# Which engine copies and stores which half of the last output tile, in a fused attention and feed-forward kernel

## The chip, the cores and the metric

The kernel runs on one core of one Trainium2 chip. The metric is device time in microseconds (us) of one execution, the median of several. The core's engines each work through their own instructions in order and meet only through semaphores: TensorE (PE in the profile; its weight loads are PEld), VectorE (DVE), ScalarE (ACT), GpSimd (POOL) and SyncE (SP). In this kernel SP does nothing but issue stores and wait; ACT computes and, towards the end, issues stores too. A row marked ACTq or SPq is the time in which that engine issues a DMA or waits, not the transfer itself.

## The reference

```python
def _attn_ref(q, k, v):                       # each (8, 12, 448, 64), float32
    scores = scale * np.matmul(q, k.transpose(0, 1, 3, 2))
    attn = softmax(scores)
    return np.matmul(attn, v)

def _moe_ref(x, w_in, w_out):                 # x (3584, 768), w_in (768, 2048), w_out (2048, 768)
    h = x @ w_in
    g = h * (1.0 / (1.0 + np.exp(-h)))
    return (g @ w_out).astype(np.float32)
```

The output of the attention, its 12 heads laid side by side, is x. The result is 3584 rows (tokens) of 768 numbers in float32.

## The kernel before, in words

Matrices are held in 16 bits; products add up in PSUM in float32. The kernel goes batch by batch through the attention, and starts the feed-forward part of a batch as soon as its x is there. What concerns us is only the very end, the second product `g @ w_out`.

That product is done in blocks of two by two: 2 x 128 rows of g with 2 halves of the 2048 inner positions, against 2 halves of the inner positions and 2 halves of 384 output columns. A scheme with seven products in place of eight is used (numbers 1, 5, 6, 2, 7, 3, 4 in the code, in this order), each of eight steps of 128 inner positions. One such block is called a quad; there are 14 of them, and `QL` (line 785) is the last, number 13. A quad makes four output tiles of 128 x 384, named by row block and column half: 00 comes from product 2's bank, 11 after product 7, 01 after product 3, and 10 after product 4, the very last product. `product` (line 788) issues the matmuls; for `QL` this is line 799, with 128 x 128 weights.

A finished tile is copied or added from its PSUM bank into an SBUF tile of the pool `ost` (four buffers, `ost` at line 825) and stored from there. Tiles 00 and 01 are copied by ACT (`take_out`, line 862, the copy itself is line 863), 11 is an addition on DVE (`add_out`, line 880, row L881). For all quads but the last, `store` (line 842) issues four DMAs of 48 KB (line 855); near the end the second and fourth of these go through ACT, the others through SP. For the last quad `store_last` (line 830) issues one DMA for a whole tile, 192 KB, at line 837, through SP unless told otherwise.

The very last tile, 10 of quad `QL`, is made in two column halves of 192 (`OQ`, line 786). `queue_quad` (line 1297), in `run` at lines 1320 to 1329, issues product 4 as two runs of eight matmuls, one for each column half, and queues one copy for each: `take_half` (line 866). Half 0 is copied by ACT (line 872) and stored through SP; half 1 is copied by DVE (line 870) and stored through ACT. Both halves lie in one PSUM bank and in one `ost` tile. This crossing matters for what follows: ACT issues the store of the half that DVE has copied, and SP issues the store of the half that ACT has copied.

The order of the instructions on each engine comes from a planner (`Order`, line 88). It keeps a clock `od.now` and a time at which each engine is free, starts the ready operation that has waited longest (with biases), and notes for each one the moment at which it was started; at the end of the kernel function (line 1742) all operations are emitted in the order of those moments. An operation's copy and its store are emitted together, since one function does both. So the planner's clock decides in which order ACT gets the two things it has to do for the last tile: the store of DVE's half, and its own copy. In the built program of the kernel before, ACT has the DMA issue of half 1 first and the copy of half 0 behind it. The waits are put in by the framework: DVE's copy (L870) waits for the last matmul of both halves, ACT's DMA issue waits for DVE's copy, ACT's copy (L872) waits for the last matmul of half 0, and SP's last store waits for ACT's copy. After its last store SP waits for every DMA of the kernel, one semaphore after the other (row L1769), and then all engines meet.

The lines that decide this, for the last product:

```python
op = Op("PE", HF * mm(OQ), lambda h=h: product(qd, m, 0, HF, h), tail=PE_OUT)
od.now += HF * mm(OQ) * x
od.on_pe(op, "full")
eng = "DVE" if x else "ACT"
read(("21", x), eng, lambda x=x: take_half(x), [op])
```

Of the kernel before, what the change touches and what calls it, by code (L numbers as in the profile page):

```python
# [30 lines left out]
def mm(n):  # L31
    return n / 2400.0 + 0.0026


def act(n):
    return n * 0.00087 + 0.13
# [151 lines left out]
def kernel(  # L188
# [9 lines left out]
    nc = tc.nc  # L198
# [410 lines left out]
    HF = NFF // 2  # L609
# [175 lines left out]
    QL = NT * B // 4 - 1  # L785
    OQ = OH // 2

    def product(qd, m, f0, f1, h=slice(0, OH)):
        a, b = 2 * qd, 2 * qd + 1
        if m in (5, 6):  # L790
            w = S_t[(qd, m - 4)]
        else:
            t, i = {1: (a, 0), 2: (a, 1), 3: (a, 1), 7: (b, 0), 4: (b, 1)}[m]
            w = rows(t, i)
        if BANK[m] == m and f0 == 0:
            pr_t[(qd, m)] = bank_m("p", qd, m)
        for f in range(f0, f1):
            if qd == QL:
                nc.tensor.matmul(  # L799
                    out=pr_t[(qd, BANK[m])][:, h],  # L800
                    lhsT=w[:, f, :],
                    rhs=W_[m][:, f, h],
                    start=(f == 0 and BANK[m] == m),
                    stop=(f == HF - 1),
                    skip_group_check=True,
                )
                continue
            wide(
                out=pr_t[(qd, BANK[m])][:, 0:OH],
                lhsT=w[:, f, :],  # L810
                rhs=W_[m][:, f, :],
                start=(f == 0 and BANK[m] == m),
                stop=(f == HF - 1),
                skip_group_check=True,
            )


    def bank(qd, m):
        return pr_t[(qd, m)][:, 0:OH]
# [5 lines left out]
    def ost(qd, i, j):  # L825
        t = sb.tile([128, OH], FP32, name=f"ost_{qd}_{i}{j}", tag="ost", bufs=NOST)
        ost_t[(qd, i, j)] = t
        return t

    def store_last(i, j, h=slice(0, OH), eng=nc.sync):  # L830
        u, t = divmod(2 * QL + i, NT)
        r, col = divmod(128 * t, S)
        b = 2 * u + r
        dst = out[b * S : (b + 1) * S, OH * j : OH * (j + 1)].rearrange(
            "(i g) m -> i g m", g=TPP
        )
        eng.dma_start(  # L837
            out=dst[:, col // 32 : col // 32 + 4, h],
            in_=ost_t[(QL, i, j)][:, h],
        )  # L840
# [18 lines left out]
    def take(qd, m):  # L859
        nc.scalar.copy(out=tmp(qd, m), in_=bank(qd, m))  # L860

    def take_out(qd, m, i, j):
        nc.scalar.copy(out=ost(qd, i, j), in_=bank(qd, m))  # L863
        store(qd, i, j)

    def take_half(x):
        h = slice(OQ * x, OQ * (x + 1))
        t = ost_t.get((QL, 1, 0)) or ost(QL, 1, 0)
        if x:
            nc.vector.tensor_copy(out=t[:, h], in_=bank(QL, 6)[:, h])  # L870
        else:
            nc.scalar.copy(out=t[:, h], in_=bank(QL, 6)[:, h])  # L872
        store_last(1, 0, h, nc.scalar if x else nc.sync)

    def add_in(qd, to, x, y):
        nc.vector.tensor_tensor(
            out=bank(qd, to), in0=bank(qd, x), in1=tmp_t[(qd, y)], op=ALU.add
        )

    def add_out(qd, m, x, i, j):  # L880
        nc.vector.tensor_tensor(  # L881
            out=ost(qd, i, j), in0=bank(qd, m), in1=tmp_t[(qd, x)], op=ALU.add
        )
        store(qd, i, j)
# [14 lines left out]
    od = Order(SHY)  # L899
# [123 lines left out]
    def in_parts(n, size, columns, emit, done, at=0):  # L1023
        to = min(at + size, n)
        op = Op("PE", (to - at) * mm(columns), lambda: emit(at, to), tail=PE_OUT)
        od.on_pe(op, "full")
        if to == n:
            done(op)
        else:
            moe.insert(  # L1030
                0, (list, 0, lambda: in_parts(n, size, columns, emit, done, to), ())
            )
# [264 lines left out]
    def queue_quad(qd):  # L1297
        quads.append(qd)
        fourth.append(qd)
        took = {}  # L1300

        def read(name, eng, fn, deps, then=None):
            busy = act(OH) if eng == "ACT" else OH / 960.0 + 0.13
            bias = B_TAKE if eng == "ACT" else B_READ
            took[name] = od.add(Op(eng, busy, fn, deps, bias, then=then))

        def out(m):
            def then(at):
                m_ring.give(at, spot[("p", qd, m)])
                ost_ring.give(at + STORE)  # L1310

            return then

        def queue(m):
            def run():
                if BANK[m] == m:
                    spot[("p", qd, m)] = m_ring.take()[0]
                for ring, need in rings:
                    ring.take(need)
                if qd == QL and m == 4:  # L1320
                    pr_op[(qd, m)] = None
                    for x in range(2):
                        h = slice(OQ * x, OQ * (x + 1))
                        op = Op("PE", HF * mm(OQ), lambda h=h: product(qd, m, 0, HF, h), tail=PE_OUT)
                        od.now += HF * mm(OQ) * x
                        od.on_pe(op, "full")
                        eng = "DVE" if x else "ACT"
                        read(("21", x), eng, lambda x=x: take_half(x), [op])
                    return
                in_parts(HF, PROD_AT, OH, lambda f0, f1: product(qd, m, f0, f1), done)  # L1330

            def done(op):
                if m == 5:
                    sg_ring.give(od.free["PE"] + PE_OUT)
                pr_op[(qd, m)] = op
                if m in (1, 5):
                    read(m, "ACT", lambda: take(qd, m), [op])
                elif m == 6:
                    read("u", "DVE", lambda: add_in(qd, 6, 6, 1), [op, took[1]], tmp_ring.give)
                    read("w", "DVE", lambda: add_in(qd, 5, 6, 5), [took["u"], took[5]])  # L1340
                elif m == 2:
                    read("11", "ACT", lambda: take_out(qd, 1, 0, 0), [op], out(1))
                elif m == 7:
                    read(
                        "22",
                        "DVE",
                        lambda: add_out(qd, 6, 5, 1, 1),
                        [op],
                        lambda at: (ost_ring.give(at + STORE), tmp_ring.give(at)),
                    )  # L1350
                elif m == 3:
                    read("12", "ACT", lambda: take_out(qd, 5, 0, 1), [op], out(5))
                else:
                    read("21", "ACT", lambda: take_out(qd, 6, 1, 0), [op], out(6))

            def deps():
                made = list(w_op.get(m, [None]))
                made += [took.get(x) for x in {2: (1,), 7: ("w",), 3: ("w",), 4: ("22",)}.get(m, ())]
                first = {5: 1, 6: 5, 7: 6, 3: 7, 4: 3}.get(m)
                if (qd, m) == (QL - 1, 4):  # L1360
                    made.append(pr_op.get((QL, 6)))
                if first:
                    made.append((pr_op.get((qd, first)), 9.0))
                elif m == 1 and qd > 0:
                    made.append((pr_op.get((qd - 1, 1)), 9.0))
                if m in (1, 2, 4):
                    t = 2 * qd + (m == 4)
                    for b in {(128 * t + c) // S for c in (0, 127)}:
                        for f in range(HF):
                            x = g_op.get((b, f + HF * (m > 1)), [None])  # L1370
                            made += [(y, f * mm(OH)) for y in x]
                    return made + ld_wout
                x = sg_op.get((qd, {5: 1, 6: 2, 7: 3, 3: 4}[m]), [])
                x = x if len(x) == 2 else [None, None]
                return made + [x[0], (x[1], 4 * mm(OH))]

            rings = ((tmp_ring, 1),) if m in (1, 5) else ((ost_ring, 1),) * (m != 6)
            moe.append((deps, int(BANK[m] == m), run, rings))

        for m in (1, 5, 6, 2, 7, 3, 4):  # L1380
            queue(m)
# [392 lines left out]
```

## Time and profile before

| what | value |
|---|---|
| median of 3 runs | 382.96 us (382.51 to 383.04) |
| the profiled execution's own time | 383.52 us |
| its span, first to last instruction | 381.5 us |
| granted TensorE clock over the span | 0.999 |
| TensorE busy | 374.3 us, 98% |
| VectorE busy | 279.8 us, 73% |
| ScalarE busy | 257.5 us, 67% |
| GpSimd busy | 85.2 us, 22% |

The span counts from the program's first instruction to its last on the core; the execution's own time is 2.0 us more, which lies around it. Busy times are sums over the whole span. The last 5 us look nothing like the rest, so the view to read for this change is the end: which engine does what after the last matmul, and what it waits for. All times of the trace below are in us from the start of the span.

### The profile page before, as it was taken

To read this page: it belongs to the slowest core of one execution; us is meant where nothing else is said; L and a number is where in the kernel's file an instruction comes from. 1 tells how busy PE (TensorE), PEld (TensorE's weight loads), DVE (VectorE), ACT (ScalarE), POOL (GpSimd) and SP (SyncE) were. 2 spreads that over 40 slices of the span, in tenths; PEclk is the share of its full clock that TensorE was granted. 3 is DMA by queue.
4 is the path that set the end of the run, shared out by engine and by line. 5 is a ranking of instruction groups with operands and counts; after the bars stand their busy time and mean duration, and the time that the engine had idled before them with its cause. 6 is when DMAs were issued, how large, how long until landed. Compare 5 with 4: busy or idle time off the path is not lost.

```text
span 381.5 us, 12934 instructions
## 1 busy us (share of the span) xinstructions
PE 374.3 (98%) x5516; PEld 192.6 (50%) x5516; DVE 279.8 (73%) x560; ACT 257.5 (67%) x425; POOL 85.2 (22%) x155
## 2 busy tenths in 40 slices
PE   8899999999999999999999999999999999999995
PEld 7433455444455444545444454555556555556663
DVE  4679799999996868997869978789866334556341
ACT  4897864887868787967788787728762259883221
POOL 7536714506042503314240500000000000000000
PEclk9999999999999999999999999999999999999999
DMA  7999999935558842739391612120002330001333
GB/s 108 195 206 181 176 210 197 164 73 90 71 99 138 140 74 41 108 65 174 80 150 26 91 25 72 33 54 0 1 4 70 82 97 2 0 1 44 103 84 103
DMA packets 35961, 34.66 MB, mean 91 GB/s; under 512 B 11968, under 2 KB 35136, under 8 KB 35904
## 3 DMA queue, kind: packets, MB, share of 16 engines
q0 software_dynamic: 25200, 22.82, 40.6%
q1 hardware_dynamic: 10176, 10.53, 10.0%
q8 instruction: 43, 0.70, 0.8%
q10 hardware_dynamic: 528, 0.49, 0.5%
q14 instruction: 14, 0.11, 0.1%
HBM read 45.61 MB, written 11.01 MB: 148 GB/s over the span
## 4 chain that ended last, share of the span: by engine, by line
PE 92%; ACT 2%; DMA 2%; POOL 1%; DVE 1%; issue 1%; ACTq 0%; POOLq 0%
PE banks L394 53%; PE banks L729 15%; PE banks L404 10%; PE banks L479 10%; ACT E L442 2%; DMA rq<-in_q_dram 2%; PE banks L799 2%; PE banks L495 2%; DMA out_dram<-ost 1%; POOL rk L309 0%; DVE T L453 0%; POOL rq L317 0%; PE banks L515 0%; DVE rq L387 0%; ACTq L837 0%
## 5 line engine op out<-in xcount | busy, mean ns | idle before, releaser
L442 ACT ACTIVATE E<-banks 128x896 f16<-128x896 f32 x168 | 144.0, 920 | 42.0 <-PE banks L404 41.7
L394 PE MATMUL banks<-xT,w_in_t 128*32 128x448 f16 (+1 forms) x1446 | 90.5, 353 | 0.0
L394 PE MATMUL banks<-w_out_t,G 128*32 128x384 f16 (+1 forms) x968 | 67.4, 327 | 0.0
L394 PEld LDWEIGHTS <-G 128*32 128x32 f16 (+1 forms) x1240 | 47.0, 97 | 34.0 <-issue 6.5
L394 PEld LDWEIGHTS <-w_in_t 128*32 128x32 f16 (+1 forms) x1446 | 42.0, 97 | 43.4 <-issue 12.7
L340 POOL DMA_DIRECT2D V<-in_v_dram x84 | 46.0, 559 | 57.1 <-PE banks L479 43.0
L404 PE MATMUL banks<-rq,KT 32*128 32x448 f16 (+1 forms) x768 | 52.5, 362 | 1.2 <-DVE rq L387 0.9
L602 ACT ACTIVATE th<-banks 128x448 f16<-128x448 f32 x72 | 37.2, 553 | 15.1 <-PE banks L394 14.4
L640 DVE SCALAR_TENSOR_TENSOR G<-th,banks 128x448 f16<-128x448 f16 (+1 forms) x72 | 39.9, 573 | 4.6 <-ACT th L602 4.3
L863 ACT COPY ost<-banks 128x384 f32<-128x384 f32 x41 | 19.8, 485 | 33.0 <-PE banks L394 17.6
L394 PE MATMUL banks<-D,S 128*32 128x384 f16 (+1 forms) x544 | 38.1, 327 | 0.0
L762 ACT ACTIVATE G<-banks 128x448 f16<-128x448 f32 (+3 forms) x72 | 33.8, 554 | 5.3 <-DVE banks L745 3.5
L479 PE MATMUL banks<-E,V 128*32 128x448 f16 x672 | 35.7, 353 | 0.0
L576 DVE SCALAR_TENSOR_TENSOR xT<-banks,rdn 128x448 f16<-128x448 f32 x48 | 29.2, 618 | 5.7 <-PE banks L479 3.0
L745 DVE TENSOR_TENSOR banks<-banks,q 128x448 f32<-128x448 f32 x28 | 17.6, 632 | 16.6 <-PE banks L729 15.4
L394 PEld LDWEIGHTS <-S 128*32 128x32 f16 (+1 forms) x544 | 20.6, 97 | 14.7 <-issue 3.1
L404 PEld LDWEIGHTS <-KT 32*128 32x128 f16 (+1 forms) x768 | 12.5, 96 | 30.7 <-issue 27.4
L453 DVE TENSOR_TENSOR T<-E,E 128x1792 f16<-128x1792 f16 x22 | 23.8, 1080 | 5.6 <-ACT E L442 5.5
L453 DVE TENSOR_TENSOR T<-T,E 128x1792 f16<-128x1792 f16 x22 | 23.9, 1086 | 5.2 <-ACT E L442 5.1
L317 POOL DMA_DIRECT2D rq<-in_q_dram x25 | 13.9, 558 | 58.1 <-PE banks L404 47.5
L479 PEld LDWEIGHTS <-V 128*32 128x32 f16 x672 | 17.0, 97 | 16.1 <-issue 3.9
L729 PEld LDWEIGHTS <-w_in_t 128*128 128x128 f16 x168 | 16.4, 98 | 15.2
(156 smaller groups left out, 402.7 us busy)
## 6 DMA issues: line engine op xcount, KB each, us to landing
out_dram<-ost SPq DMA_DIRECT2D x200, 48.0 KB, 1.6
rk<-in_k_dram POOLq DMA_DIRECT2D x23, 224.0 KB, 5.4
rq<-in_q_dram POOLq DMA_DIRECT2D x23, 224.0 KB, 5.2
w_out_t<-in_moe_w_out_dram POOLq DMA_DIRECT2D x4, 768.0 KB, 13.4
V<-in_v_dram POOLq DMA_DIRECT2D x42, 64.0 KB, 3.9
V<-in_v_dram POOLq DMA_DIRECT2D x42, 48.0 KB, 4.4
w_in_t<-in_moe_w_in_dram POOLq DMA_DIRECT2D x3, 512.0 KB, 10.5
w_in_t<-in_moe_w_in_dram POOLq DMA_DIRECT2D x6, 256.0 KB, 6.5
```

The lines of the kernel that those rows point to most:

```text
L340: nc.gpsimd.dma_start(out=v_of(b, hg0)[32 * x : 32 * (x + 1), at, 0:count, :], in_=v[b, hs].rearrange("h (i g) d -> i h g d", g=TPP)[:, :, ...
L394: nc.tensor.matmul(out=out[at], lhsT=lhsT[:, at], rhs=rhs, **flags)
L404: nc.tensor.matmul(out=pS[p0 : p0 + 32 * (x1 - x0), h % 2, at : at + nq], lhsT=KT[(b, hg)][32 * h : 32 * (h + 1), c, x0:x1, :, e], rhs=QT[ ...
L442: nc.scalar.activation(out=E[(n, w)][0:kr, 2 * y : 2 * y + 2, 0:nk], in_=pS_t[(n, w, y)][0:kr, :, 0:nk], func=AF.Exp, scale=attn_scale,)
L453: nc.vector.tensor_tensor(out=T[n], in0=T[n] if step else E[(n, 0)], in1=E[(n, step + 1)], op=ALU.add,)
L479: nc.tensor.matmul(out=a[32 * h : 32 * (h + 1), 0:nq], lhsT=w, rhs=e[k0:k1, h, at : at + nq], start=start, stop=stop,)
L576: nc.vector.scalar_tensor_tensor(out=x3(b, cc)[:, cc % 3, 32 * g0 : 32 * g1], in0=acc[(n, part)][:, 0:nq], scalar=0.5, in1=rdn_t[n].rearra ...
L602: nc.scalar.activation(out=th, in_=h_t[(b, f, t0)][:, 0 : t1 - t0], func=AF.Tanh)
L640: nc.vector.scalar_tensor_tensor(out=dst[:, f, at + lo : at + hi], in0=th_t[(b, f, t0)][:, lo - t0 : hi - t0], scalar=1.0, in1=h_t[(b, f, ...
L729: nc.tensor.matmul(out=pp_t[(f, PBANK[m])], lhsT=w[:, c, :], rhs=a[:, c, :], start=(c == 0 and m in (1, 6, 5)), stop=(c == 2), skip_group_ ...
L762: nc.scalar.activation(out=o, in_=a, func=AF.Silu, scale=2.0)
L863: nc.scalar.copy(out=ost(qd, i, j), in_=bank(qd, m))
```

## The change

The engines of the two halves are exchanged, and the planner's clock is no longer moved on between the two runs of matmuls: the second run's time is added to the moment at which that run counts as done. The matmuls, the sizes of the copies and the sizes of the stores stay as they are.

```diff
@@ take_half
         if x:
+            nc.scalar.copy(out=t[:, h], in_=bank(QL, 6)[:, h])
+        else:
             nc.vector.tensor_copy(out=t[:, h], in_=bank(QL, 6)[:, h])
-        else:
-            nc.scalar.copy(out=t[:, h], in_=bank(QL, 6)[:, h])
         store_last(1, 0, h, nc.scalar if x else nc.sync)
@@ queue_quad, run
                         op = Op("PE", HF * mm(OQ), lambda h=h: product(qd, m, 0, HF, h), tail=PE_OUT)
-                        od.now += HF * mm(OQ) * x
                         od.on_pe(op, "full")
-                        eng = "DVE" if x else "ACT"
+                        op.done += HF * mm(OQ) * x
+                        eng = "ACT" if x else "DVE"
                         read(("21", x), eng, lambda x=x: take_half(x), [op])
```

Now half 0 is copied by DVE (line 872 of the changed kernel) and stored through SP, and half 1 is copied by ACT (line 870) and stored through ACT. In the built program of the changed kernel every engine has as many instructions as before, and all stand in the same order but these: ACT has its copy first and its DMA issue behind it. DVE's copy waits for the last matmul of both halves, as before. SP's last store waits for DVE's copy. ACT's copy waits for DVE's copy. ACT's DMA issue waits for ACT's copy.

## Prediction

> **What bounds the kernel now.** I read the page first, to see which engine carries the span, then the chain of waits over the end, since the edit touches the last two copies and the last two stores alone.
>
> ```profile
> span 381.5 us, 12934 instructions
> PE 374.3 (98%) x5516; PEld 192.6 (50%) x5516; DVE 279.8 (73%) x560; ACT 257.5 (67%) x425; POOL 85.2 (22%) x155
> ```
>
> TensorE is busy for 98% of the span. The order of the instructions in the built programs is the same in both kernels up to the last copies, so everything up to the last matmul should take the same time. What can move is the end. The chain of waits there, in order of time (start, duration, what):
>
> ```profile
> 374.25 0.57 DVE ost L881
> 374.81 0.02 issue
> 374.83 2.11 DMA out_dram<-ost
> 376.94 0.35 DVE ost L870
> 377.29 0.02 issue
> 377.31 0.65 ACTq L837
> 377.96 0.04 issue
> 378.00 0.02 ACTq L872
> 378.02 0.04 issue
> 378.06 0.32 ACT ost L872
> ```
>
> Three pieces of work follow each other here: DVE copies half 1 (L870), ACT spends 0.65 us issuing the store of that half (ACTq L837), and only then does ACT copy half 0 (L872). The chain stops at the last computing instruction; what comes behind it is the last store on SP and the wait for it. The next rows give the matmuls of the last product and the wait in front of DVE's copy, each from the view of its line (count, shortest/median/longest ns, first and last start), and then DVE's copy and SP's issues from the timeline (start, duration, engine, and in brackets the idle time before):
>
> ```profile
> L799 PE MATMUL banks<-D,G x16: 246/246/246, 375.3 to 376.6; 128*128 128x192 f16 x16
> ```
>
> ```profile
> L870 DVEq EVENT_SEMAPHORE  x2: 21/1202/2383, 374.3 to 374.5; - x2
> ```
>
> ```profile
> 376.92 0.36 DVE L870 COPY ost<-banks 128x192 f32<-128x192 f32 x1 [2.12 <-DMA out_dram<-ost]
> ```
>
> ```profile
> 376.05 2.89 SPq L837 DMA_DIRECT2D out_dram<-ost  x2
> ```
>
> ```profile
> 378.40 0.54 SPq L837 DMA_DIRECT2D out_dram<-ost  x1
> ```
>
> The chain blames a DMA for DVE's start, the store of tile 11 issued at 374.83. A view of that store alone contradicts it:
>
> ```profile
> L837 SPq DMA_DIRECT2D out_dram<-ost x1: 550/550/550, 374.8 to 374.8; - x1
> ...
> DMA to landing us min/median/max: 2.2/2.2/2.2
> ```
>
> That store landed at 374.83 + 2.2 = 377.0, after the copy had begun at 376.92. The last of the 16 matmuls starts at 376.6 and takes 0.246, so it ends at about 376.8. DVE's wait began at 374.5 and lasted 2.383, to 376.9. So the matmuls released DVE, both halves of them, and this does not change.
>
> Last, the landings in the window from 376 on (issue, count, size, us from the issue's start to landing), what SP waited for at the end (in all, times, longest), and the last 1.1 us (busy time of PE, PEld, DVE, ACT, POOL, then clock, DMA share and GB/s):
>
> ```profile
> out_dram<-ost SPq DMA_DIRECT2D x1, 192.0 KB, 2.3
> out_dram<-ost ACTq DMA_DIRECT2D x1, 96.0 KB, 2.1
> out_dram<-ost SPq DMA_DIRECT2D x1, 96.0 KB, 2.0
> ```
>
> ```profile
> SPq L837 <- ACT ost L872: 1.7, 1, 1.7
> SPq L1769 <- DMA out_dram<-ost: 1.1, 2, 0.9
> ```
>
> ```profile
> 380.40:381.50 1.10, 0.00 (x0) 0.00 (x0) 0.00 (x0) 0.00 (x0) 0.00 (x0) 0.68 0.00 0
> ```
>
> The last store is SP's, issued at 378.40 and landed 2.0 later, at 380.40. SP then has its closing waits, and the span ends 1.1 us after that landing, with no engine computing and no DMA running (last row). So the end of the kernel is: last matmul, DVE's copy, ACT's issue, ACT's copy, SP's issue and landing, 1.1 us of closing.
>
> **The change, part by part.** The sum is made against the profiled execution: 383.52 us, of which 381.5 are the span and 2.0 lie around it. That execution is 0.56 above the median of 382.96; the difference worked out below is taken off the median.
>
> *DVE's copy.* It now reads half 0 in place of half 1. It is still 128 x 192, and still waits for all 16 matmuls, so it stays at 376.92 with 0.36 and ends at 377.28. It cannot go earlier, although half 0's matmuls are done some 0.7 sooner (sixteen start between 375.3 and 376.6, and half 0 has the first eight), because the wait covers both halves. Cost zero.
>
> *SP's last store.* It now waits for DVE's copy and not for ACT's. SP issued the store before it at 376.05 and took 0.55 (the 0.550 of the equal store above), so it is free from 376.6. DVE's end to the next issue took 0.03 before (377.28 to 377.31), so SP issues at 377.31, and 2.0 later, at 379.3, half 0 has landed. That is 1.1 earlier than before.
>
> *ACT's copy.* It no longer stands behind the 0.65 us issue, but it waits for DVE's copy. It starts at 377.28 plus 0.03, at 377.31, in place of 378.06, and with 0.32 ends at 377.63. Behind it on ACT stands only ACT's own store, and for that waits only the closing of SP.
>
> *ACT's store.* Issued 0.03 later, at 377.66, by the engine that made the data. It is now the last of the two. Before, the last issue was at 378.40: 0.74 later. ACT's store took 2.1 from issue to landing, SP's 2.0, for the same 96 KB; ACT's issue itself lasted 0.65 against 0.54. I keep 2.1 for ACT, the row of the same DMA on the same queue: it lands at 377.66 + 2.1 = 379.76, against 380.40.
>
> *The closing.* SP waits for the same set of semaphores, with three waits and the meeting of the engines behind the last landing, as before; I keep 1.1. Sum: 380.40 - 379.76 = 0.64 us less. The span becomes 380.9, the profiled execution's time 382.88, and the median 382.96 - 0.64 = **382.3 us**, 0.17% less.
>
> *The unknown.* What the trace doesn't show is one 96 KB store on ACT issued 0.35 after one on SP. From below: ACT's landing is as short as SP's, 2.0, and 0.74 are won. From above, the nearest rows are stores of 48 KB that SP and ACT issued in pairs, 373.4 to 373.9, SP's landings first and ACT's second:
>
> ```profile
> DMA to landing us min/median/max: 1.5/1.6/1.7
> ```
>
> ```profile
> DMA to landing us min/median/max: 1.8/1.8/1.8
> ```
>
> ```profile
> 373.45 0.79 SPq L855 DMA_DIRECT2D out_dram<-ost  x2
> 373.45 0.86 ACTq L855 DMA_DIRECT2D out_dram<-ost  x2
> ```
>
> Issued side by side, ACT's landed 0.2 later than SP's, at the medians. If that much is added to 2.1, the store lands at 379.96 and 0.44 are won. The data themselves hardly meet. In equal slices of 0.104 from 377.31 on, the bytes moved are:
>
> ```profile
> GB/s 426 338 367 412 206 30 0 0 0 0 0 0 88 301 338 191 22 0 0 0 0 15 257 316 280 74 0 0 0 0 0 0 0 0 0 0 0 0 0 0
> ```
>
> Half 1, issued at 377.31, moves in slices 13 to 17, from 1.25 to 1.8 after its issue. Half 0, issued at 378.40, moves in slices 22 to 26, from 1.1 to 1.6 after its issue. Each needs under 0.5 us on an otherwise idle set of engines. With issues at 377.31 and 377.66, the second's data begin about when the first's end. The first six slices are the store of tile 01, which is through by 377.94, before either. That is why I take the value nearer to no contention.
>
> **A rule of the Trainium skill at this place.** In the list of all waits the row for ACT's copy is:
>
> ```profile
> ACT ost L872 <- DVE ost L870: 2.0, 1, 2.0
> ```
>
> Before, this wait came by way of the DMA issue in front of the copy; afterwards it is a wait of the copy itself. The Trainium skill's page "PSUM — Partial Sum Buffer", section "PSUM bank collisions raise a hardware error", says that two engines must not be in the same bank and quadrant at one time, reads against reads included. By that rule the two copies of this bank can't run side by side, and the sum stays at 382.3; without it the first rival would be open. The built program agrees with the rule, as far as order goes; no run here shows a collision. The page "DMA: Bandwidth & Descriptors", section "Issuing engines are not separate DMA queues", speaks against the second half of the edit: issuing on two engines saves only the time to issue. By that rule, and with SP's 0.54, the gain of ACT's own issue would be the 0.19 between 377.66 and 377.85, when SP would be free again; the other 0.55 come from the order on ACT.
>
> **The rivals.**
>
> *More is won.* If the copies ran side by side, ACT's copy would start at 376.92, its store at 377.27, and land at 379.37; SP's would land at 379.31. Then 380.40 - 379.37 = 1.03 are won: 381.9 us. Against it stands ACT's wait for DVE in the built program. The weaker form, a landing of 2.0, gives 0.74 and 382.2. Chance of the two together 0.15, nearly all of it for the weaker.
>
> *Contention at the end.* ACT's second store pays the 0.2 of the pairs: 382.5 us. For it, the pairs; against it, the idle DMA engines. Chance 0.09.
>
> *It doesn't matter.* Something other than the last landing ends the span, such as a closing that is a fixed time after the last matmul; or the edit leaves the order as it was, which the built program excludes. SP's wait of 0.9 for a DMA, just before the closing, speaks against it. 382.96 us, chance 0.02.
>
> *Slower.* The last store moves from SP's queue, which has carried nearly all stores, to ACT's, right behind a store on SP's. If its landing stretches, the gain goes: it is gone at 2.74 from issue to landing, and at 3.5 the kernel is slower by over 0.2%. Landings do stretch in this kernel; over all stores of line 855 the row is
>
> ```profile
> DMA to landing us min/median/max: 1.5/1.7/5.8
> ```
>
> A middle case of 3.7 gives 377.66 + 3.7 = 381.36, 0.96 later than before: 383.9 us. Against it: long landings need traffic, and after 377.94 there is none but the two halves. Chance 0.06. The forecast has the remaining 0.68.
>
> **How the numbers follow.** A measurement of this kernel can tell about 0.2% from no change, 0.77 us. The three runs lie 0.53 apart, so a difference of two medians may be off by some 0.3. The forecast of 0.64 is only 0.13 short of 0.77, so of its 0.68 about 0.45 fall on faster, the rest within, with 0.02 of it slower: 0.31, 0.36, 0.01. *More is won* gives 0.12 and 0.03, contention 0.01 and 0.07 and 0.01, no effect 0.02 within, the slow case 0.06. Together: faster 0.44, within 0.2% 0.48, slower 0.08. The range takes the gains from 0.44 to 0.74 with 0.3 of scatter on either side, 381.92 to 382.82, and 0.2 more at each end for the stronger forms of *more is won* and of contention: 381.7 to 383.0. Left out are the slow case and the tails.
>
> **What would show it.** In the changed kernel's profile: DVE's copy 0.1 after the last matmul, as before; SP's last issue right at DVE's end; ACT's copy 0.03 to 0.05 after DVE's end, then ACT's issue; both issues begun within 0.4 us of each other; the last landing 2.1 after ACT's issue and 2.9 after the last matmul's end, against 3.6 before; and 1.1 from there to the end. The prediction is wrong if ACT's landing takes over 2.4, if ACT's copy starts before DVE's ends, or if the time up to the last matmul moves.

## The result and the profile after

The changed kernel takes 382.32 us (median of 12 runs, 382.06 to 383.03); the kernel before, over the 12 runs that stand beside it, 383.08 us (382.51 to 384.16). The ratio is 0.9977, with a 95% interval of 0.9967 to 0.9988: faster by 0.23%, and by at least 0.12% at the near end of that interval. 382.3 was predicted.

The page of the changed kernel, first row and busy times:

```profile
span 380.5 us, 12933 instructions
...
PE 373.5 (98%) x5516; PEld 192.0 (50%) x5516; DVE 280.2 (74%) x560; ACT 257.6 (68%) x425; POOL 85.3 (22%) x155
```

The chain of waits over the end, in order of time (start, duration, what):

```profile
373.85 0.57 DVE ost L881
374.42 0.02 issue
374.43 2.10 DMA out_dram<-ost
376.54 0.35 DVE ost L872
376.89 0.02 issue
376.91 0.32 ACT ost L870
```

Before, there were three pieces of work after DVE's copy had begun: the copy, ACT's 0.65 us issue, ACT's copy. Now there are two copies, 0.02 apart by the chain (0.03 by the timeline below), and the issue has left the chain. As before, the DMA named ahead of DVE's copy is not what released it. The timeline has the matmuls end at 374.94 + 1.48 = 376.42, and DVE's copy start 0.10 after that, the same distance as in the kernel before:

```profile
374.94 1.48 PE L799 MATMUL banks<-D,G 128*128 128x192 f16 x16
375.14 0.48 ACT L863 COPY ost<-banks 128x384 f32<-128x384 f32 x1 [2.12 <-PE banks L799]
376.52 0.36 DVE L872 COPY ost<-banks 128x192 f32<-128x192 f32 x1 [2.12 <-DMA out_dram<-ost]
376.91 0.32 ACT L870 COPY ost<-banks 128x192 f32<-128x192 f32 x1 [1.29 <-DVE ost L872]
377.26 0.66 ACTq L837 DMA_DIRECT2D out_dram<-ost  x1
```

SP's last issue, from the timeline of SP alone, and the landings from 375.9 on (us from issue to landing at the end of each row):

```profile
376.90 0.54 SPq L837 DMA_DIRECT2D out_dram<-ost  x1
```

```profile
out_dram<-ost SPq DMA_DIRECT2D x1, 192.0 KB, 2.3
out_dram<-ost SPq DMA_DIRECT2D x1, 96.0 KB, 2.0
out_dram<-ost ACTq DMA_DIRECT2D x1, 96.0 KB, 2.1
```

Half 0 lands at 378.9, half 1 at 377.26 + 2.1 = 379.36. From there to the end nothing computes and no DMA runs (busy times, then clock, DMA share, GB/s):

```profile
379.37:380.46 1.09, 0.00 (x0) 0.00 (x0) 0.00 (x0) 0.00 (x0) 0.00 (x0) 0.51 0.00 0
```

The two profiled executions differ by 1.0 us in span, more than the end explains. The trace's records give the last matmul's end as 376.83 before and 376.43 after, so 0.40 came earlier than the edit, and from the last matmul to the end of the span it is 4.66 before and 4.03 after: 0.63 is what the edit moved. Where the 0.40 lies can be read too. The first row is the kernel before, the second the changed kernel, the third experiment e2, whose instructions are those of the changed kernel, all at the same stretch of ACT's exponentials:

```profile
12.63 4.16 ACT L442 ACTIVATE E<-banks 128x896 f16<-128x896 f32 x5 [1.58 <-PE banks L404]
```

```profile
12.00 4.96 ACT L442 ACTIVATE E<-banks 128x896 f16<-128x896 f32 x6 [0.29 <-PE banks L404]
```

```profile
11.73 4.96 ACT L442 ACTIVATE E<-banks 128x896 f16<-128x896 f32 x6 [0.28 <-PE banks L404]
```

The executions part in the first 13 us, where the first loads land, and then run in step for 350 us: matmul by matmul the changed kernel stays 0.67 ahead of the kernel before. It gives 0.27 of that back at 368. There ACT's copy of a tile waits for an older store to clear its buffer, with 2.33 us of idle time in the kernel before (first row) and 2.75 in the changed kernel (second row). In the changed kernel TensorE then needs the bank that ACT is to free, and its next matmul starts 0.05 after that copy ends:

```profile
368.17 0.48 ACT L863 COPY ost<-banks 128x384 f32<-128x384 f32 x1 [2.33 <-DMA out_dram<-ost]
```

```profile
367.92 0.48 ACT L863 COPY ost<-banks 128x384 f32<-128x384 f32 x1 [2.75 <-DMA out_dram<-ost]
```

Neither place is touched by the edit, and both programs have the same instructions there. Nor is the beginning the only place: e2, first of the three at 12 us, falls 0.52 behind the changed kernel's pace near 68 us, where its matmuls wait for a chain of VectorE work behind a load, and its last matmul ends at 376.53. So the time of one execution carries up to a microsecond that has nothing to do with the end, and what the end does is best read from the last matmul on.

### The profile page after: what moved, and what is told of

It reads as the page before. It is cut to its first block, busy times and chain, and to the rows that moved or that the text cites. A ratio compares the mean times of both kernels' runs of the same rounds, so it can differ in the third digit from the quotient of the medians.

```text
span 380.5 us, 12933 instructions
## 1 busy us (share of the span) xinstructions
PE 373.5 (98%) x5516; PEld 192.0 (50%) x5516; DVE 280.2 (74%) x560; ACT 257.6 (68%) x425; POOL 85.3 (22%) x155
## 4 chain that ended last, share of the span: by engine, by line
PE 92%; ACT 3%; DMA 2%; DVE 1%; issue 1%; POOLq 0%
PE banks L394 53%; PE banks L729 15%; PE banks L404 11%; PE banks L479 10%; ACT E L442 3%; PE banks L495 2%; PE banks L799 1%; DMA out_dram<-ost 1%; DMA rk<-in_k_dram 1%; PE banks L1673 0%; DVE ost L881 0%; DVE T L453 0%; PE banks L515 0%; DVE KT L377 0%; DVE rq L387 0%
```

## The experiments

Two columns of the table are from the trace's records of instructions and landings, counted from the end of the last matmul: the last landing and the end of the span. They don't contain the scatter of the beginning. The medians and ratios do; each ratio is against the kernel before, run beside it on the same chip (medians 383.14 for e1, e3, e4, e5, which ran on one chip, and 383.21 for e2, e6, e7, e8, which ran on another). The medians are of 12 runs, but of 11 for e3, e4 and e8, of 7 for e5 and of 6 for e6.

| kernel | last landing | end of span | median us | ratio (95%) |
|---|---|---|---|---|
| before | 3.56 | 4.66 | | |
| changed | 2.93 | 4.03 | 382.32 | 0.9977 (0.9967 to 0.9988) |
| e1, planner's line alone | 2.87 | 3.98 | 382.29 | 0.9982 (0.9974 to 0.9990) |
| e2, exchange alone | 2.93 | 4.03 | 382.48 | 0.9984 (0.9970 to 0.9998) |
| e3, both stores on SP | 3.10 | 4.21 | 382.35 | 0.9985 (0.9972 to 0.9999) |
| e4, one copy, one store | 2.76 | 3.93 | 382.37 | 0.9978 (0.9967 to 0.9988) |
| e5, two banks | 2.48 | 3.59 | 381.77 | 0.9965 (0.9952 to 0.9977) |
| e6, ACT's second store | 2.83 | 3.93 | 382.18 | 0.9970 (0.9959 to 0.9981) |
| e7, e5 and e6 | 2.37 | 3.48 | 382.18 | 0.9977 (0.9961 to 0.9994) |
| e8, split by rows | 3.43 | 4.54 | 383.13 | 0.9998 (0.9988 to 1.0009) |

**e1: the planner's line alone.** The edit has two parts; this one keeps the engines as they were.

```diff
                         op = Op("PE", HF * mm(OQ), lambda h=h: product(qd, m, 0, HF, h), tail=PE_OUT)
-                        od.now += HF * mm(OQ) * x
                         od.on_pe(op, "full")
+                        op.done += HF * mm(OQ) * x
                         eng = "DVE" if x else "ACT"
```

> The planner's line alone is changed; the engines keep their halves (ACT half 0, DVE half 1). In the built program ACT now has its copy ahead of its DMA issue, and DVE's copy waits for ACT's copy. Theory (the gain is the order on ACT: no DMA issue in front of a copy): last matmul's end + 0.04 + 0.32 (ACT) + 0.04 + 0.36 (DVE) + 0.03 to ACT's issue, some 0.8 us, and the landing 2.1 later, 2.9 us after the last matmul, as in the changed kernel; 0.6 us below the kernel before. Rival (the gain is that the engine that copies a half also issues its store): ACT still issues DVE's half, so the time stays at that of the kernel before, 3.6 us from the last matmul to the last landing.

The end of its chain, and ACT's issue from its timeline:

```profile
373.42 2.63 PE banks L799 x24
376.05 0.02 issue
376.08 0.33 ACT ost L872
376.40 0.02 issue
376.43 0.36 DVE ost L870
```

```profile
376.82 0.66 ACTq L837 DMA_DIRECT2D out_dram<-ost  x1
```

The copies have changed places, ACT first and DVE second, and the sum is the same: 2.87 to the last landing. ACT still issues the store of the half that DVE copied, so the rival falls: nothing is won by copying and storing on the same engine. What matters is that no copy stands behind an issue. (The 0.05 against the changed kernel is the first start: ACT's copy starts 0.04 after the last matmul where DVE's starts 0.09 after it.)

**e2: the exchange of engines alone.**

```diff
+                        od.now += HF * mm(OQ) * x
                         od.on_pe(op, "full")
-                        op.done += HF * mm(OQ) * x
                         eng = "ACT" if x else "DVE"
```

(against the changed kernel)

> The engines are exchanged, but the planner's clock is moved on as in the kernel before. In the built program every engine has the same instructions in the same order with the same waits as in the changed kernel. Theory (the time follows from the instructions alone): the changed kernel's time, 0.6 us below the kernel before, with 2.9 us from the last matmul to the last landing; what its median differs from the changed kernel's is the scatter of the measurement, up to 0.3 us. Rival (the planner's line is worth something by itself): not possible in a program with the same instructions, so a difference over 0.4 us would mean that the scatter has been taken too small.

2.93 and 4.03, as the changed kernel to the hundredth; medians 382.48 and 382.32. So each half of the edit alone brings the gain, and the second adds nothing. The medians of one and the same program lie 0.16 apart, taken in different sessions.

**e3: both stores through SP.**

```diff
-        store_last(1, 0, h, nc.scalar if x else nc.sync)
+        store_last(1, 0, h, nc.sync)
```

> The changed kernel, but both halves' stores go through SP. Theory (order on ACT; the queue is a small part): SP issues half 0 at 0.48 after the last matmul's end, takes 0.54, and issues half 1 at about 1.07 in place of 0.83; with a landing of 2.0 in place of 2.1 the last one lands at 3.05 after the last matmul in place of 2.93. 0.1 us above the changed kernel, 0.5 us below the kernel before. Rival (a second queue is what gains): the two stores run one after the other, half 1 lands 2.0 after half 0's landing begins to clear, 3.6 us or more after the last matmul, and the gain is gone.

The two landings are equal, and the second issue starts 0.63 after the first, at 376.50:

```profile
377.13 0.55 SPq L837 DMA_DIRECT2D out_dram<-ost  x1
```

```profile
out_dram<-ost SPq DMA_DIRECT2D x2, 96.0 KB, 2.0
```

The last landing is at 3.10, 0.18 after that of the changed kernel (0.12 was expected; SP spends 0.09 and not 0.05 between its two issues, on a wait of its own, and 1.07 + 2.0 is 3.07 and not 3.05). The rival fails: the second queue saves 0.18, no more. It lets the last issue start 0.28 earlier (0.83 against 1.11 after the last matmul), and ACT's landing gives 0.10 of that back. That the saving is less than one issue of 0.54 agrees with the Trainium skill's page "DMA: Bandwidth & Descriptors", section "Issuing engines are not separate DMA queues", by which a second issuing engine saves only the time to issue.

**e4: one copy, one store.** ACT copies the whole last tile, and SP stores it.

```diff
         if x:
-            nc.scalar.copy(out=t[:, h], in_=bank(QL, 6)[:, h])
-        else:
-            nc.vector.tensor_copy(out=t[:, h], in_=bank(QL, 6)[:, h])
-        store_last(1, 0, h, nc.scalar if x else nc.sync)
+            nc.scalar.copy(out=t, in_=bank(QL, 6))
+            store_last(1, 0)
```

> The changed kernel, but the last tile is copied whole by ACT (128 x 384) and stored whole through SP (192 KB); the matmuls are still in two runs. Theory (the two copies run one after the other, so the split wins nothing): 0.04 + 0.48 (ACT's 128 x 384 copy) + 0.03 to the issue, and 2.25 to landing as the other 192 KB stores took; 2.8 us after the last matmul, 0.1 below the changed kernel and 0.75 below the kernel before. Rival (halves hide part of the copy and the transfer): the whole tile costs the 0.48 and the longer transfer with nothing beside it, and it is slower than the changed kernel by 0.2 to 0.4 us.

The end of its chain, and the landing:

```profile
373.47 2.15 PE banks L799 x21
375.62 0.02 issue
375.64 0.48 ACT ost L870
```

```profile
out_dram<-ost SPq DMA_DIRECT2D x1, 192.0 KB, 2.2
```

One copy of 0.48 in place of 0.36 + 0.03 + 0.32, and a landing of 2.22 in place of 2.09: 2.76, as the theory had it. The rival, by which the whole tile is slower, is wrong for this program: a half lands 0.13 sooner after its issue, but that issue starts 0.29 later. The changed kernel's split costs 0.1 (end of span) to 0.17 (last landing) while both copies wait for all matmuls and then for each other. Not all of this belongs to the split: 0.05 of it is that DVE's first copy starts later than ACT's, and e6 below, which is split too, ends at the same 3.93.

**e5: two banks.** The halves of the last tile's accumulator are put into two PSUM banks. Products 6 and 7 of the last quad are issued in column halves too.

```diff
-            pr_t[(qd, m)] = bank_m("p", qd, m)
+            pr_t[(qd, m)] = PB_[:, 0:2, 0:OQ] if (qd, m) == (QL, 6) else bank_m("p", qd, m)
         for f in range(f0, f1):
+            if qd == QL and BANK[m] == 6:
+                for y in (0, 1) if m != 4 else (h.start // OQ,):
+                    nc.tensor.matmul(
+                        out=pr_t[(qd, 6)][:, y],
+                        lhsT=w[:, f, :],
+                        rhs=W_[m][:, f, OQ * y : OQ * (y + 1)],
...
-            nc.scalar.copy(out=t[:, h], in_=bank(QL, 6)[:, h])
+            nc.scalar.copy(out=t[:, h], in_=bank(QL, 6)[:, 1])
```

> The changed kernel, but the two column halves of the last tile's accumulator lie in two PSUM banks, so that products 6 and 7 of the last quad are also issued as halves (16 more matmuls, 192 columns each in place of 384). In the built program DVE's copy waits for half 0's matmuls alone, and ACT's copy for half 1's alone, not for DVE. Theory (what is left is the chain last matmul, copy, copy, issue): half 0 is copied and stored while half 1's matmuls run; ACT's copy starts 0.04 after the last matmul, ends at 0.36, issue at 0.39, landing 2.1 later at 2.5 us, 0.43 less than the changed kernel; about 0.04 is given back for the extra matmuls, so 0.4 below the changed kernel and 1.0 below the kernel before. Rival (the end is set by the DMA alone or by the closing, and copies hide beside each other already): no change from the changed kernel.

From its timeline, DVE's copy and ACT's, and from its chain the last matmuls (line numbers are that kernel's own):

```profile
376.26 0.36 DVE L890 COPY ost<-banks 128x192 f32<-128x192 f32 x1 [1.46 <-PE banks L800]
```

```profile
376.86 0.32 ACT L888 COPY ost<-banks 128x192 f32<-128x192 f32 x1 [0.84 <-PE banks L800]
377.21 0.66 ACTq L855 DMA_DIRECT2D out_dram<-ost  x1
```

```profile
375.51 1.33 PE banks L800 x16
376.84 0.02 issue
376.86 0.32 ACT ost L888
```

DVE's copy now runs from 376.26 to 376.62, while half 1's matmuls are still going on to 376.83, and ACT's follows the last of them by 0.04. The last landing comes at 2.48, as expected, and the end 0.44 earlier than in the changed kernel. The 16 extra matmuls lie ahead of the point from which this is counted. They cost the expected 0.04: from the start of an ACT copy that lies ahead of product 6 to the last matmul's end it is 12.98 in e5 and 12.94 in the kernel before, so about 0.40 is left of the gain. The median is 381.77, 0.55 below the changed kernel's; the two intervals of the ratios overlap, so the order of these two is shown by the trace and only made likely by the times. Against the kernel before, 0.35% (0.23% to 0.48%) is clear.

**e6: ACT's second store.** Tile 01's store goes through ACT, ahead of the last copy, where ACT is idle.

```diff
         if qd == QL:
-            store_last(i, j)
+            store_last(i, j, eng=nc.scalar if (i, j) == (0, 1) else nc.sync)
             return
```

> The changed kernel, but the whole-tile store of tile 01 goes through ACT too, so that ACT's last store is its second of this shape (line 837) and not its first. Theory A (the 0.65 us of ACT's issue, and its landing of 2.1 against SP's 2.0, belong to the first DMA of a shape on a queue; SP's first also took 0.64): ACT's last issue takes 0.55 and lands after 2.0, 0.1 us less than the changed kernel. Theory B (ACT's issues are slower as such): it stays at 0.65 and 2.1. By both, the added issue on ACT ends 0.6 us before ACT's copy can start, so it costs nothing; if an issue on ACT cost time wherever it stands, the time would be 0.6 us above the changed kernel.

```profile
375.24 0.66 ACTq L837 DMA_DIRECT2D out_dram<-ost  x1
376.50 0.32 ACT L870 COPY ost<-banks 128x192 f32<-128x192 f32 x1 [1.29 <-DVE ost L872]
376.85 0.55 ACTq L837 DMA_DIRECT2D out_dram<-ost  x1
```

```profile
out_dram<-ost ACTq DMA_DIRECT2D x1, 96.0 KB, 2.0
```

The timeline of ACT shows both of its issues, 0.66 and 0.55. The second lands after 2.00 in place of 2.09, and the end is 0.10 earlier, as theory A has it. The rows also answer what an issue on ACT costs: ACT is idle for 0.6 us after the added one, and the copy starts where it did. Here an issue costs time only where a copy is ready behind it.

**e7: e5 and e6 together.**

> The two changes together: the halves of the last tile's accumulator in two banks, and tile 01's store through ACT. Theory A: the last landing comes 2.4 us after the last matmul in place of 2.48 with two banks alone, 1.2 us below the kernel before. Theory B: 2.48, 1.1 us below. If the added issue on ACT, at 0.8 to 0.1 us before the last matmul, stood in the way of ACT's copy, 0.1 to 0.2 us more.

Last landing at 2.37, the end at 3.48, 1.18 below the kernel before: the shortest end of all, by theory A. Its median, 382.18, was taken on another chip and is above e5's 381.77, with intervals of the ratio that overlap (0.9961 to 0.9994, 0.9952 to 0.9977). From the last matmul on it is shorter by 0.11; whether it is also faster in time, these runs can't say.

**e8: split by rows.** DVE copies rows 0 to 63, ACT rows 64 to 127, all columns.

```diff
-        h = slice(OQ * x, OQ * (x + 1))
+        r = slice(64 * x, 64 * (x + 1))
...
-            nc.scalar.copy(out=t[:, h], in_=bank(QL, 6)[:, h])
+            nc.scalar.copy(out=t[r], in_=bank(QL, 6)[r])
...
-        store_last(1, 0, h, nc.scalar if x else nc.sync)
+        store_last(1, 0, eng=nc.scalar if x else nc.sync, ws=(2 * x, 2 * x + 2))
```

> The changed kernel, but the last tile is split by rows: DVE copies rows 0 to 63 with all 384 columns, ACT rows 64 to 127, and each half is stored by the same queue as in the changed kernel. In the built program ACT's copy still waits for DVE's. Theory (a copy's time goes by its columns and the two run one after the other): 0.09 + 0.56 (DVE, 384 columns) + 0.04 + 0.48 (ACT) + 0.03 to ACT's issue, 1.2 us in place of 0.83; last landing 3.3 us after the last matmul, 0.35 above the changed kernel and 0.3 below the kernel before. Rival (a copy's time goes by its elements): the copies take what they take in the changed kernel, and so does everything, 2.9 us.

```profile
376.25 0.55 DVE L872 COPY ost<-banks 64x384 f32<-64x384 f32 x1 [2.12 <-DMA out_dram<-ost]
```

```profile
376.83 0.47 ACT L870 COPY ost<-banks 64x384 f32<-64x384 f32 x1 [1.48 <-DVE ost L872]
377.33 0.65 ACTq L837 DMA_DIRECT2D out_dram<-ost  x1
```

```profile
out_dram<-ost SPq DMA_DIRECT2D x1, 96.0 KB, 2.2
out_dram<-ost ACTq DMA_DIRECT2D x1, 96.0 KB, 2.3
```

With half the rows and twice the columns the copies take 0.55 and 0.47, what 384 columns on all 128 rows took (0.56 for an addition on DVE, 0.48 for a copy on ACT). So two copies in a row, each the length of a whole one, follow the last matmul. The rival falls. The landing was a miss of mine: the same 96 KB in 64 rows took 2.2 and 2.3 in place of 2.0 and 2.1, so the last landing is at 3.43 and not 3.3. In time it is the kernel before (0.9988 to 1.0009), with 0.12 less at the end.

## Why the prediction was right

*DVE's copy doesn't move.* Right: 0.09 after the last matmul in both kernels, although it reads the half that is done 0.66 earlier. e5 shows what this wait costs: with half 0 in a bank of its own, the copy ran under the matmuls.

*SP's store right behind DVE's copy.* Right: issued 0.03 after the copy's end, landed after 2.0.

*ACT's copy 0.03 behind DVE's, then its issue.* Right: 0.03, 0.32, 0.03; the issue starts 0.83 after the last matmul against a forecast of 377.66 - 376.83 = 0.83.

*ACT's landing 2.1.* Right: 2.09. The dearer end, 2.3, taken from the pairs of 48 KB stores, didn't come about, although the two issues overlapped by 0.18 (377.26 to 377.44). The data themselves came one after the other, as the prediction expected. In 40 slices from 376.9 to 379.4 of the changed kernel's trace, the last two groups of numbers are half 0 and half 1, which meet at 378.5 to 378.6:

```profile
GB/s 344 369 393 369 393 369 369 246 123 0 0 0 0 0 0 0 0 0 0 135 246 369 307 295 185 37 37 184 344 344 319 234 99 12 0 0 0 0 0 0
```

e6 names what the 0.1 between ACT's landing and SP's was: it goes away when ACT has issued a store of this form shortly before.

*The closing, 1.1.* Right: 1.10 in both, and 1.10 to 1.16 in all the experiments, while the last landing moved from 3.56 to 2.37. So the last landing does end the span, and *it doesn't matter* falls.

*The sum.* 0.64 was worked out; the end measures 0.63 shorter. The medians differ by 0.76, with an interval from 0.46 to 1.26 (0.12% to 0.33% of 383.08), so they agree with 0.63 but do not sharpen it. That the median came out at 382.32, to the hundredth what 382.96 - 0.64 gives, is luck: the kernel before has 383.08 over 12 runs and not the 382.96 of the first three, and the medians differ by 0.76 and not by 0.64. In the same sense the sign is settled and the bound of 0.2% is not: 0.23% stands at the middle of the interval, and the end alone gives 0.16%.

*A sign of being wrong that came up.* The prediction names three, and one of them is that the time up to the last matmul moves. It moved by 0.40, from 376.83 to 376.43. The traces don't lay this to the edit: the two part in the first 13 us, on instructions that are the same in both, and traces that share those instructions differ by more among themselves (e2's matmuls end at 376.53, e4's at 375.60). But the kernel before has one trace only, and its matmuls end later than those of the seven others that have the same matmuls, so the traces alone don't settle that it is chance. The times of e8 speak for chance. Its end is 0.12 shorter than that of the kernel before, and its median 0.08 lower. A lasting 0.40 on top would be 0.52, or 0.14%, just outside its interval (0.12% faster to 0.09% slower). The sign was a poor one: the spans of the changed kernel's own twelve runs go from 380.0 to 381.0.

*The causes.* The prediction ascribed 0.19 of the 0.74 by which the last issue comes earlier to the second queue and 0.55 to the order on ACT. e3 measures 0.18 for the queue at the last landing, which leaves 0.45 of the 0.63 for the order. That 0.18 stands so near 0.19 is in part luck. The prediction left out SP's 0.09 between two issues, which makes the queue worth 0.28 at the issue, and it left the 0.10 by which ACT's landing is longer out of this division; the two nearly cancel. e1 shows that the order alone gives the whole when the second queue is kept.

*More is won* did not happen; e5 is the form in which copies really do run beside other work, and it brings a further 0.44 from the last matmul on. *Slower* did not happen either. The reason given against it, that long landings need traffic, stands up in the trace of the kernel before. By its packet records, 110 of the 208 stores of line 855 had neither loads nor instruction fetches moving beside them, and these landed within 1.87 us; all 73 that took over 2 us had one or the other. The traffic can be little: four stores issued at 364.4 to 364.8 took 3.1 to 3.3 us, and all that moved beside the stores in that stretch is one packet of instructions, 16 KB, which took 1.29 us:

```profile
q8 instruction: 1, 0.02, 3.7%
...
out_dram<-ost SPq DMA_DIRECT2D x2, 48.0 KB, 3.1
out_dram<-ost ACTq DMA_DIRECT2D x2, 48.0 KB, 3.2
```

That the packet delayed them is likely and was not tested. Up to the last landing of the changed kernel no such packet stands beside its two last stores.

*The rule of the skill.* The Trainium skill's page "PSUM — Partial Sum Buffer", section "PSUM bank collisions raise a hardware error", says that two engines in one bank and quadrant at a time raise an error. The programs keep clear of it: one bank, and the copies wait for each other (changed kernel, e1, e8); two banks, and the wait is gone (e5). What this shows is where the framework puts waits, not a collision. By the page, different quadrants of one bank do not collide; in e8 the rows lay in different quadrants and the framework still made ACT wait. Copies side by side in one bank without that wait weren't tried, by columns or by rows, so no run here shows what they would do.

## What to carry to other kernels

In all traces here ACT does its copies and its DMA issues one after the other, in the order of its program. So at the end of a kernel one looks for a copy that stands behind the store of another engine's data: here that cost 0.65 us of issue and could be had for one line of the planner. Splitting the last tile paid only where the halves could be worked on apart: in one PSUM bank the split ended 0.1 later than a single copy (and level with it in e6), in two banks 0.34 earlier, or 0.30 with the extra matmuls counted. For changes of this size, count from the last common event in the trace, since the times themselves scatter by as much as the change is worth.

## What the runs showed of the hardware

- ACT's store of half 1 took 0.65 to 0.66 us to issue and 2.09 to land where it was ACT's first store of line 837 (changed kernel), and 0.55 and 2.00 where it was the second (e6, and in e7 0.55 and 1.99). SP's first took 0.64 to 0.65, its later ones 0.54 to 0.56. What costs the 0.1, that it is the first of its form or a pause before it, was not tested by itself. The pauses speak against the second: SP's last store in the kernel before came 1.81 after SP's previous issue had ended and took 0.54, ACT's first in e6 came 1.76 after ACT's and took 0.66. But the two are different engines.
- A store of 96 KB landed after 2.0 to 2.1 as 128 rows of 768 bytes, and after 2.2 to 2.3 as 64 rows of 1536 bytes; 192 KB in 128 rows took 2.2 to 2.3 on SP, and 2.4 as ACT's first store (e6, e7).
- Of the scatter between executions, most of what could be traced arose in the first 13 us, while the first loads landed: the eight profiled executions that have the same matmuls lie up to 1.2 us apart there. Six of them keep their distance to the last matmul within 0.03; e2 loses 0.52 near 68 us, the changed kernel 0.27 at 368.
